# Loading q ahead of the raw token weights and rounding them between the first tiles' statistics, in an attention and MLP-mixer kernel

## The chip, the cores and the metric

The kernel runs on one core of one Trainium2 chip. The metric is the device time of one execution in microseconds (us). The core has a matrix engine (TensorE, PE in the profile), a vector engine (VectorE, DVE), an activation engine (ScalarE, ACT), GpSimd (POOL) and SyncE (SP), which here only issues transfers. "PEld" is the loading of weights into TensorE. Each engine runs its own instructions in order and waits on semaphores for the others. Transfers (DMA) are issued from a queue of SP, ScalarE or GpSimd and run on 16 DMA engines.

## The reference

```
kv  = einsum('bhsd,bhse->bhde', k, v)            # 8 batches, 8 heads, 576 rows, head size 64
o   = einsum('bhsd,bhde->bhse', q, kv)
o   = o / sqrt(mean(o*o, last axis) + 1e-6) * g_norm
x   = o, heads side by side                      # (8, 576, 512)
u   = x + (relu(x^T @ w_tok1) @ w_tok2)^T        # token mixing, 576 -> 256 -> 576
out = u + relu(u @ w_ch1) @ w_ch2                # channel mixing, 512 -> 1536 -> 512
```

The inputs q, k, v and g_norm are 32-bit floats; the four weights arrive as 64-bit floats and are rounded to 32 bits on the chip.

## The kernel before

The batches are worked on in four pairs. A pair has two sides, its two batches. A first stage (`start`) does the attention and part of the token mixing of pair 0. A second one (`middle`) finishes the token mixing of pair 0 beside the attention of pair 1. Two more (`steady`) and `last` follow in the same way, and after them comes the channel mixing, which takes most of the time. The change lies in the loads ahead of `start`, in `start` and in the first lines of `middle`.

The order of work is written out by hand. `start` and `middle` are lists of strings with short names of steps. `play` takes the names one by one and calls each step's function, and every instruction goes through `keep`, which holds it in that order on its engine. So on each engine the order of the strings is the order of execution. The names that matter here, with a tile c of two row blocks t (c = 0 and 1 are the two halves of side 0's 512 rows, 2 and 3 those of side 1, 4 the remainder, the last 64 rows of both sides):

- `kv{side}{half}`: k transposed times v for four of the eight heads, into PSUM (ps_kv, L133); `e{side}{half}` copies it to SBUF (kvp): on VectorE (L383) for side 0 of pair 0, otherwise on ScalarE (L130).
- `a{c}{t}`: q times kvp into a PSUM bank (ps_o, or ps_r for the remainder); there are two such banks in use.
- `g{c}{t}`: the bank times g_norm into x on VectorE (L444); `q{c}{t}`: its square on ScalarE (L448); `t{c}{t}`: the sum over a head on VectorE (L465); `m{c}`, `r{c}`, `i{c}`: mean (L470, VectorE), root (L475, ScalarE) and the inverse with one correction step (L479 to L484, four instructions on VectorE).
- `d{c}{t}` and `s{c}{t}`: x times that inverse, as one instruction on VectorE (L502) or as eight on ScalarE (L498).
- `h{side}{t}{j}`: one product of the first token weight, block t, with row block j of x, summed in a PSUM bank (ps_h); `h10` and `h11` are all four row blocks of side 1; `hr` is the part of the remainder, and the relu (L127) of all follows it.
- `w{n}{k}`: the rounding of weight block n. Blocks 0 and 1 are the two halves of w_tok1, 2 is its remainder, 3 and 4 are w_tok2. k = 0 loads the raw 64-bit words; 1 is two activations on ScalarE (L163 writes the scaled high word, L166 scales the low word in place); 2, 3 and 4 are a clamp (L169), a shift (L173) and an exact addition (L178) on VectorE.
- `j{n}`: n products of the identity with itself (ps_j) that nothing reads. They keep TensorE running.
- `l{side}{half}`, `lq`, `lr`: loads for the next pair, issued from SP.

A product of 32-bit floats is two passes in the profile. The loads of k, v, q and the raw weights are issued from SP in order (the first two of v from ScalarE). `load(n)` fetches k and v for half the heads of a batch, each as a transfer of 512 KB and one of 64 KB; `load_q(b)` fetches 1 MB of q; a raw block of w_tok1 is 512 KB. The transfers of the hardware queues use eight semaphores in turn, so one waits until that of eight places ahead has landed.

Of the kernel before, what the change touches and what calls it, by code (L numbers as in the profile page):

```python
# [20 lines left out]
def kernel(  # L21
# [90 lines left out]
    def do(f, *a, **kw):  # L112
        return lambda: f(*a, **kw)
# [6 lines left out]
    def dma(o, i, engine=nc.sync):  # L120
        keep(engine.dma_start(o, i))
# [16 lines left out]
    def load(n):  # L138

        if n >= 2 * B:  # L140
            return
        cols = [t[n // 2, :, ts(n % 2, DH)] for t in (k, v)]

        queues = (nc.sync, nc.scalar if n < 2 else nc.sync)
        for dst, c, e in zip((k_in[n % 4], v_in[n % 4]), cols, queues):
            dma(dst[:, :J], c[:LO].rearrange("(j p) e -> p j e", p=P), e)
            dma(dst[:HF, J], c[LO:], e)

    def load_q(b):
        if b < B:  # L150
            qT[b] = qtp.tile([P, HP, LO], F32, name="qT", tag="qT", bufs=2)
            dma(qT[b], q[b].rearrange("(c p) s -> p c s", p=P)[..., :LO])
# [69 lines left out]
    def get_ch2(f):  # L222

        a = 2 * (2 * f // NS)

        def loads(raw):
            t = raw.rearrange("p (h f n) w -> p f h n w", h=2, f=2)
            rows = words(moe_w_ch2)[ts(f, 2 * P)].rearrange("(f p) (h n) w -> f p h n w", f=2, h=2)
            return [(t[:, i], rows[i]) for i in range(2)]

        dst = w_ch2[:, a:a + 2, ds(2 * f % NS, 2)]
        return block(2 * DM, loads, dst.rearrange("p h f n -> p h (f n)"))
# [19 lines left out]
    def t_sums(b):  # L252

        def step(o, x, y):
            return lambda: tensor_add(b(o), b(x), b(y), ALU.subtract)

        return [step(5, 7, 1), step(6, 3, 5), step(7, 3, 7), step(4, 2, 6)]
# [934 lines left out]
    def play(lines, after={}, **stages):  # L1192

        for name in " ".join(lines).split():
            if name.isdigit():
                for _ in range(int(name)):
                    next(stages["rounding"], lambda: None)()
            elif name[0] == "-":  # L1200
                stages["before"][name[1:]]()
            else:
                next(stages[s][name] for s in ("attention", "mixing", "more")
                     if name in stages.get(s, ()))()
# [4 lines left out]
    channel = ([get_ch1(c, f) for f in range(2) for c in range(NC)]  # L1209
               + [get_ch2(f) for f in range(NF // 2)])  # L1210
    load(0)
    for block in tok1[:2]:
        block[0]()
    load(1)
    for t in [t for pair in zip(k_in, v_in) for t in pair]:
        keep(nc.gpsimd.memset(t[HF:, J], 0.0))
    zeroed = [ps["kv"].tile([P, 2, P], F32, name="ps_kv", tag="kv") for _ in range(2)]
    for t in zeroed:
# [5 lines left out]
    make_identity(nc, ident)  # L1224
    dma(g_sb, bass.AP(tensor=g_norm.tensor, offset=g_norm.offset,
                      ap=[[0, P], [0, 1], list(g_norm.ap[0])]), nc.scalar)
    load_q(0)
    for n in range(2, 4):
        load(n)
    load_q(1)  # L1230
# [2 lines left out]
    for block in tok1[2:] + tok2:  # L1233
# [5 lines left out]


    start = [
        "kv00 e00 l00 j14 w01 w11 w02 w03 w04 w12 w13 w14", "kv01 j10 e01 l01",
        "a00 g00 q00", "a01 g01 q01 t00 t01 m0", "a10 q10 r0 i0 d00 d01", "a11 q11 g10 g11 t10",
        "kv10 e10 t11 m1 r1", "h000 h010 h001", "kv11 e11 i1 d10 s11", "h011", "a20 q20",
        "a21 q21 g20 g21 t20 t21 m2", "h002 h012 r2 i2 d20", "a30 q30 g30", "a31 q31 s21 g31 t30", "h003 h013 t31 m3",
        "a40 q40 r3 i3 d30 s31 g40 t40 m4 r4 w21 i4 s40 lq0 l10 l11 lr0 lr1"]
    middle = [
        "kv00 e00 w31 w22 w23 w24", "h10 -lq1 w32 w33 w34", "kv01 e01 w41 w42",
        "h11 w43 w44", "hr l00", "a0 q00 g01 q01 g00 t00 t01", "u0 z2 f0", "u1 l01",
        "a1 q10 g11 q11 g10 t10 t11 m0 r0 lq0", "u2 i0", "kv10 e10 z4 d00", "u3 s01", "kv11 e11",  # L1250
        "u4 z6 f1", "a2 q20 g21 q21 g20 s10", "u5 t20 t21 f2", "a4 q40 g41 q41 g40 lr0 lr1 1", "u6 t40 t41 1 l10",
        "a3 q30 g31 q31 g30 lq1 d11", "u7 t30 t31 m2 r2 1 i2 p20 p21 s30", "u8 1 l11 d31"]
# [17 lines left out]
    more = {f"w{n}{k}": f for n, b in enumerate(tok1 + tok2) for k, f in enumerate(b)}  # L1270
# [6 lines left out]
    def keep_warm(n):  # L1277

        o = ps["h"].tile([P, DM], F32, name="ps_j", tag="h")
        for _ in range(n):  # L1280
            matmul(o[:, :P], lhsT=ident, rhs=ident, start=True, stop=True)

    more |= {f"j{n}": do(keep_warm, n) for n in (10, 14)}
    play(start, attention=attentions[0], mixing=mixings[0], more=more)
    play(middle, attention=attentions[1], mixing=mixings[0], before=attentions[0],
         more=more, rounding=rounding)
    for n in range(1, B // 2 - 1):
        play(steady[n - 1], attention=attentions[n + 1], mixing=mixings[n], before=attentions[n],
             more=more, rounding=rounding)
# [16 lines left out]
    more = {f"c{i}": f for i, f in enumerate(t_sums(lambda n: uT[0][:, SB[n]]))}  # L1306
# [97 lines left out]
```

## Time and profile before

| | |
|---|---|
| median of 3 runs | 788.1 us (786.69 to 788.41) |
| profiled execution, its own time | 787.48 us |
| its span | 785.7 us |
| TensorE busy | 773.3 us (98%) |
| VectorE busy | 614.8 us (78%) |
| ScalarE busy | 269.5 us (34%) |
| GpSimd busy | 71.3 us (9%) |
| granted TensorE clock | 1.0 |
| read from and written to HBM | 138.31 MB, 52.82 MB |

The span is the time from the first to the last instruction that the profile shows; the execution's own time is 1.8 us more. Busy shares are averages over the whole span. The first 60 us, with which the change has to do, look otherwise:

| stretch, us | PE busy | DVE busy | ACT busy | GB/s |
|---|---|---|---|---|
| 0 to 10 | 3.80 | 1.03 | 1.68 | 258 |
| 10 to 20 | 9.00 | 4.63 | 2.88 | 330 |
| 20 to 30 | 9.51 | 7.99 | 4.54 | 311 |
| 30 to 40 | 9.78 | 8.20 | 5.94 | 326 |
| 40 to 50 | 9.80 | 6.45 | 8.22 | 324 |
| 50 to 60 | 10.00 | 7.91 | 5.51 | 342 |

A row of the timeline gives start, duration, engine, line, operation, the tile written and the tiles read, shapes, how many instructions were merged, and in brackets how long the engine had been idle before and what ended the wait. The chain of waits is followed back from the last instruction: each piece is what the next one had to wait for.

### The profile page before, as it was taken

The numbers are of one execution on the slowest core, as the hardware profiler recorded it, in microseconds if no ns is written. First come the engines' busy times: TensorE is split into PE (matmuls) and PEld (weight loads), VectorE is DVE, ScalarE is ACT, GpSimd is POOL, SyncE is SP. The second block draws the span as 40 slices with busy tenths as digits, with TensorE's granted clock in tenths as the row PEclk, the third lists the DMA queues.
The fourth block names the chain that finished last, engine by engine and source line by source line (L and its number), as shares of the span: only waits on it lengthen the run. The fifth ranks groups of instructions, "written<-read, shape, count | busy, mean of one in ns | idle before, by whom it ended". The sixth has DMA issues, their size and how long they took to land.

```text
span 785.7 us, 14826 instructions
## 1 busy us (share of the span) xinstructions
PE 773.3 (98%) x5816; PEld 651.6 (83%) x5816; DVE 614.8 (78%) x909; ACT 269.5 (34%) x531; POOL 71.3 (9%) x84
## 2 busy tenths in 40 slices
PE   6999999999999999999999999999999999999998
PEld 6655545545888888999988899998889999889998
DVE  2877887795776868988778889776998885787977
ACT  2567463845110233521134242123352113325211
POOL 1001112123410000010100001010000101000111
PEclk9999999999999999999999999999999999999999
DMA  9999999787699795598897579889559989655864
GB/s 294 318 330 374 362 360 325 268 267 285 239 286 343 268 329 161 162 294 215 234 248 225 147 216 277 247 200 291 150 154 280 221 213 236 196 150 157 197 171 91
DMA packets 132613, 192.12 MB, mean 245 GB/s; under 512 B 13632, under 2 KB 92224, under 8 KB 132544
## 3 DMA queue, kind: packets, MB, share of 16 engines
q1 hardware_dynamic: 115984, 167.54, 67.8%
q0 software_dynamic: 14656, 22.02, 13.8%
q10 hardware_dynamic: 1904, 1.61, 0.7%
q8 instruction: 46, 0.75, 0.4%
q14 instruction: 23, 0.19, 0.1%
HBM read 138.31 MB, written 52.82 MB: 243 GB/s over the span
## 4 chain that ended last, share of the span: by engine, by line
PE 92%; ACT 3%; DVE 2%; DMA 2%; issue 0%; SPq 0%; ACTq 0%; DVEq 0%
PE ps_d L133 28%; PE ps_b L133 19%; PE ps_a L133 19%; PE ps_u L133 7%; PE ps_h L133 6%; PE ps_v L133 5%; PE ps_c L133 3%; PE ps_w L133 2%; PE ps_o L133 2%; PE ps_kv L133 2%; DMA raw<-in_moe_w_tok_dram 1%; ACT x L498 1%; DMA raw<-in_moe_w_ch_dram 1%; DVE ms L465 1%; DVE x L444 1%; ACT sq L448 1%
## 5 line engine op out<-in xcount | busy, mean ns | idle before, releaser
L133 PE MATMUL ps_d<-ui,w 128*128 128x256 f32 x504 | 118.7, 379 | 0.0
L130 ACT COPY ps_d<-ps_a 128x768 f32<-128x768 f32 (+1 forms) x56 | 32.0, 571 | 215.3 <-PE ps_a L133 215.3
L133 PEld LDWEIGHTS ps_d<-ui,w 128*128 128x128 f32 x504 | 95.1, 190 | 12.8 <-DVE v L124 0.2
L124 DVE TENSOR_TENSOR v<-v,v 128x1536 f32<-128x1536 f32 (+2 forms) x70 | 103.5, 1483 | 0.3
L133 PE MATMUL ps_b<-w,sv 128*128 128x128 f32 x672 | 84.6, 276 | 0.0
L133 PE MATMUL ps_a<-w,v 128*128 128x128 f32 x672 | 84.2, 275 | 0.0
L133 PEld LDWEIGHTS ps_a<-w,v 128*128 128x128 f32 x672 | 79.8, 192 | 0.2
L133 PEld LDWEIGHTS ps_b<-w,sv 128*128 128x128 f32 x672 | 79.5, 192 | 0.2
L133 PE MATMUL ps_u<-h,w_tok 128*128 128x512 f32 (+1 forms) x160 | 67.2, 606 | 0.8 <-ACT ps_u L130 0.7
L133 PE MATMUL ps_h<-x,w_tok 128*128 128x512 f32 (+1 forms) x160 | 65.6, 604 | 0.6 <-DVE x L502 0.4
L133 PE MATMUL ps_d<-w,v 128*128 128x128 f32 x528 | 66.2, 275 | 0.0
L133 PEld LDWEIGHTS ps_d<-w,v 128*128 128x128 f32 x528 | 62.7, 192 | 0.3
L127 ACT ACTIVATE v<-v 128x768 f32<-128x768 f32 (+1 forms) x54 | 42.6, 822 | 55.1 <-DVE v L124 55.1
L133 PE MATMUL ps_d<-w,sv 128*128 128x128 f32 x480 | 60.1, 275 | 0.0
L133 PEld LDWEIGHTS ps_d<-w,sv 128*128 128x128 f32 x480 | 57.1, 192 | 0.2
L133 PEld LDWEIGHTS ps_h<-x,w_tok 128*128 128x128 f32 (+1 forms) x160 | 26.0, 189 | 32.8 <-issue 27.6
L133 PEld LDWEIGHTS ps_u<-h,w_tok 128*128 128x128 f32 (+1 forms) x160 | 24.8, 179 | 31.5 <-issue 25.9
L1121 POOL DMA_DIRECT2D out_dram<-us x11 | 14.2, 1292 | 381.2 <-ACT us L130 268.9
L133 PE MATMUL ps_a<-uT,w 128*128 128x256 f32 x192 | 46.7, 379 | 0.0
L133 PE MATMUL ps_b<-ui,w 128*128 128x256 f32 x168 | 40.8, 379 | 0.0
L133 PEld LDWEIGHTS ps_a<-uT,w 128*128 128x128 f32 x192 | 36.3, 190 | 4.8
L444 DVE TENSOR_TENSOR x<-ps_o,g_sb 128x512 f32<-128x512 f32 x32 | 21.4, 687 | 23.7 <-PE ps_o L133 15.6
(145 smaller groups left out, 1213.0 us busy)
## 6 DMA issues: line engine op xcount, KB each, us to landing
w<-parts SPq DMA_DIRECT2D x168, 384.0 KB, 4.0
w<-parts SPq DMA_DIRECT2D x56, 192.0 KB, 3.0
uT<-blocks SPq DMA_DIRECT2D x36, 256.0 KB, 5.7
k_in<-in_k_dram SPq DMA_DIRECT2D x16, 512.0 KB, 9.0
qT<-in_q_dram SPq DMA_DIRECT2D x8, 1024.0 KB, 9.5
out_dram<-x POOLq DMA_DIRECT2D x16, 512.0 KB, 6.5
v_in<-in_v_dram SPq DMA_DIRECT2D x14, 512.0 KB, 9.1
raw<-in_moe_w_ch_dram SPq DMA_DIRECT2D x8, 768.0 KB, 10.5
```

Source lines behind the costliest of these rows:

```text
L124: keep(engine.tensor_tensor(out=o, in0=a, in1=b, op=op))
L127: keep(nc.scalar.activation(o, a, AF.Relu))
L130: keep(nc.scalar.copy(o, a))
L133: keep(nc.tensor.matmul(*a, **kw))
L444: keep(nc.vector.tensor_mul(x, bank[c, h], g_sb.to_broadcast([P, number(c), D])))
L448: keep(nc.scalar.activation(sq[c, h], bank[c, h], AF.Square))
L465: keep(nc.vector.tensor_reduce(stats_of(c)[0][:, h], sq[c, h], axis=AX.X, op=ALU.add))
L498: keep(nc.scalar.activation(x[:, k, h], x[:, k, h], AF.Copy, scale=inv[:, k, h]))
L1121: keep(nc.gpsimd.dma_start(to.rearrange("t p e -> p t e"), a, accum_op=ALU.add))
```

## The change

Ahead of `start`, the second k and v and the first q are loaded before the two raw blocks of w_tok1 in place of behind them.

In `start`, the rounding of the two halves of w_tok1 moves from the first line to between the statistics of tile 0 and tile 1. Row block 1 of tile 0 is scaled on ScalarE (`s01`) in place of VectorE (`d01`). The second group of identity products has 8 in place of 10, and a third group of 16 stands ahead of the first product with w_tok1. `kv10` moves behind that product.

In `middle`, `kv00` and `kv01` of pair 1 with their copies move from ahead of `h10` and `h11` to behind both, next to the remainder `hr`. The rounding steps beside them stay in order.

```diff
     load(0)
+    load(1)
+    load_q(0)
     for block in tok1[:2]:
         block[0]()
-    load(1)
...
-    load_q(0)
     for n in range(2, 4):
         load(n)
...
     start = [
-        "kv00 e00 l00 j14 w01 w11 w02 w03 w04 w12 w13 w14", "kv01 j10 e01 l01",
-        "a00 g00 q00", "a01 g01 q01 t00 t01 m0", "a10 q10 r0 i0 d00 d01", "a11 q11 g10 g11 t10",
-        "kv10 e10 t11 m1 r1", "h000 h010 h001", "kv11 e11 i1 d10 s11", "h011", "a20 q20",
-        "a21 q21 g20 g21 t20 t21 m2", "h002 h012 r2 i2 d20", "a30 q30 g30", "a31 q31 s21 g31 t30", "h003 h013 t31 m3",
+        "kv00 e00 l00 j14", "kv01 e01 l01 j8", "a00 g00 q00", "a01 g01 q01 t00 t01 m0 w01",
+        "a10 w02 w03 r0 q10 i0 d00 w04 w11", "a11 q11 s01 w12 w13 w14 j16", "h000", "kv10 e10 g10 g11 t10 t11 m1 r1",
+        "h010 h001 h011", "kv11 e11 i1 d10 s11", "a20 q20", "a21 q21 g20 g21 t20 t21 m2", "h002 h012 r2 i2 d20",
+        "a30 q30 g30", "a31 q31 s21 g31 t30", "h003 h013 t31 m3",
         "a40 q40 r3 i3 d30 s31 g40 t40 m4 r4 w21 i4 s40 lq0 l10 l11 lr0 lr1"]
     middle = [
-        "kv00 e00 w31 w22 w23 w24", "h10 -lq1 w32 w33 w34", "kv01 e01 w41 w42",
-        "h11 w43 w44", "hr l00", "a0 q00 g01 q01 g00 t00 t01", "u0 z2 f0", "u1 l01",
+        "h10 -lq1 w31 w22 w23 w24 w32", "h11 w33 w34 w41 w42", "kv00 kv01 e00 e01 w43 w44", "hr l00", "a0 q00 g01 q01 g00 t00 t01", "u0 z2 f0", "u1 l01",
...
-    more |= {f"j{n}": do(keep_warm, n) for n in (10, 14)}
+    more |= {f"j{n}": do(keep_warm, n) for n in (8, 14, 16)}
```

## The prediction

> **What bounds the kernel now.** First the page, for who is busy and what the last chain consists of:
>
> ```profile
> span 785.7 us, 14826 instructions
> PE   6999999999999999999999999999999999999998
> PE 92%; ACT 3%; DVE 2%; DMA 2%; issue 0%; SPq 0%; ACTq 0%; DVEq 0%
> ```
>
> TensorE is full in every slice but the first. Between 42 us and the end its single passes leave only three gaps over 0.1 us: 0.24 at 69.3, 0.12 at 105.9 and 0.66 at 148.7. So a delay before 42 us should reach the end nearly whole, and all edits of work lie there. Second, the chain of waits of the first 60 us (start, us, what):
>
> ```profile
> 2.49 9.63 DMA raw<-in_moe_w_tok_dram
> 12.14 0.68 ACT w_tok L163
> 12.84 0.71 DVE w_tok L178
> ...
> 13.95 1.39 PE ps_kv L133 x40
> 15.33 2.43 PE ps_j L133 x20
> ...
> 23.11 0.70 DVE x L502
> ...
> 23.86 2.84 PE ps_h L133 x6
> 26.70 1.32 PE ps_kv L133 x40
> ...
> 39.51 2.03 ACT x L498 x8
> ...
> 41.58 1.12 PE ps_h L133 x2
> ```
>
> It begins with the raw token weights and ends with the last scaling, s31 (39.51), for which `h10`'s fourth tile waits. Between 30.95 and 41.5 only VectorE and ScalarE carry it. The 13.95 is laid to L178; the k of `kv01` was issued at 6.12 and took 7.7 us, so it landed at 13.86 and held `kv01`. Third, the timeline of the two places that decide; TensorE beside the remainder and ScalarE ahead of the second pair of tiles:
>
> ```profile
> 36.29 1.09 PE L133 MATMUL ps_r<-kvp,qR 128*64 128x128 f32 x16 [0.22 <-DVE x L444]
> 37.22 1.35 PE L133 MATMUL ps_kv<-v_in,k_in 128*64 128x64 f32 x40
> 38.50 2.88 PE L133 MATMUL ps_h<-x,w_tok 128*128 128x512 f32 x6
> 41.58 1.12 PE L133 MATMUL ps_h<-x,w_tok 128*128 128x512 f32 x2 [0.20 <-ACT x L498]
> 42.63 1.39 PE L133 MATMUL ps_kv<-v_in,k_in 128*64 128x64 f32 x40
> ```
>
> ```profile
> 28.06 0.37 ACT L130 COPY kvp<-ps_kv 128x256 f32<-128x256 f32 x1 [0.81 <-PE ps_kv L133]
> 28.33 2.02 ACT L498 ACTIVATE x<-x,inv 128x64 f32<-128x64 f32 x8
> 30.25 1.30 ACT L448 ACTIVATE sq<-ps_o 128x512 f32<-128x512 f32 x2
> ```
>
> Pair 1's `kv00` (37.22) fills time in which `h10` would wait anyway: only 0.20 us is idle at 41.58. ScalarE does e11, s11, q20 in a row, and e11 starts when `kv11` ends.
>
> [...]`ps_j` passes start 0.213 us apart until 11.5 us, 0.112 after.[...] From 3 to 6 us the two queues had 50.0% and 57.7% of the engines[...].
>
> **The change, step by step.** *q in front.* SP's queue is now k0, k1, q0, raw0, raw1. `kv00` (6.20) and the 14 `ps_j` matmuls to 13.40 stand as before: k0 and v0 are first in both queues. v1 is untouched on ScalarE's queue and landed by 2.76+8.4 = 11.2. k1 takes raw0's place, which landed at 1.87+7.9 = 9.8. Both are before 13.40, so `kv01` starts there: -0.55. The 8 `ps_j` that follow instead of 10 save 2x0.223 = 0.45. So `a00` starts at 16.60 in place of 17.59: -0.99. q landed at 16.7 with 1 MB of raw ahead; at the 329 GB/s of this stretch that is 3.2 us, so now about 13.5. Were it as late as 16.7, a00 would lose 0.1; were k1 as late as 13.9, 0.5. raw0 and raw1, 1 MB behind q, land by about 16.7, before their use at 19.8. The loads k2 to q1 each wait for the landing of the DMA eight places ahead (eight semaphores are used in turn) and come at the same times within a us; their users start 5 us later. I take 0 for that.
>
> *Rounding between statistics.* It was seven VectorE instructions at 10.51 to 15.27, free under the warming matmuls; now it has to come before `h000`. Up to m0 all moves by -0.99: g00 17.70, q01 19.32, m0's end 20.84, a11's end on TensorE 21.06. VectorE: w02 and w03 (0.43 each) to 21.76, the four steps of i0 (22.12 to 23.08 before) from 21.79, d00 at 22.78, w04 (0.70) from 23.39 to 24.09. ScalarE: w01 19.83 to 21.06, r0 and q10 to 21.70; then w11. In the built program its L163 waits for w04's L178 (both write `w_tok1`), so it runs 24.12 to 25.36, and behind it stand q11 (to 25.86), s01 (8 activations, 2.02, to 27.79), e10, r1, e11, s11. s01 replaces d01, 0.6 us of VectorE. VectorE then does w12 to w14 until 26.52, g10, g11, t10, t11 (2.5 us) and i1, until d10's end at 31.09.
> TensorE: 16 `ps_j`, 32 passes of 0.112 and 0.1 to begin, fill 21.06 to 24.73, 0.64 beyond w04. Without them h000 could start at 24.13; the wait for w04 would stand there in their place. h000 0.96, `kv10` 1.31 (it filled the wait for d00 before), h010, h001, h011 2.77 (as 23.86 to 26.63), `kv11` from 29.77: its end is 31.2 where it was 28.06. h010's wait (w14) and h001's (s01, 27.79 against 27.96) are just covered; if s01 is 1 us later, 0.8 is lost there.
> e11 31.21, s11 31.48 to 33.50, q20 33.40, g20 34.01 against 30.86: +3.15. q21 no longer trails a21: -0.1. From there to s31 instructions and order are the same, so `h10`'s fourth tile starts at 41.58+3.05 = 44.63.
>
> *kv00 and kv01 of the second pair.* Both now come behind `h11`. Their time is the same, but kv00's 1.32 us leaves the wait for s31 and comes after it. The remainder starts at 39.3 (g30), `h10` waits about 1.2 us for d30 and 0.4 for s31; nothing is left to put there. +1.32. Were TensorE the late one there, it would be 0. e00 and e01 go behind w31, w41 on ScalarE, with `hr` (2.07 us) between them and `a0`: 0. The later k_in reload waits for kv00 (about 50 in place of 38.5), but SP comes to it at 48.7 only, so 1 to 2 us on a load used near 100: 0. One raw block of the channel weights goes behind a uT load near 164 on SP, for a rounding with slack: 0 to 0.3.
>
> Sum: 3.05+1.32 = +4.37. Less what the gap of 0.66 at 148.7 takes up, which follows a load on saturated DMA: 0 to 0.66, I take 0.3. +4.1 us on the profiled execution's 787.48 us (span 785.7 and 1.8 around it): 791.6. The median of the three runs is 788.1, so 792.2.
>
> **The rivals.** A, the sum: 792.2 (791.6 to 792.7), 0.66. B, the stage is TensorE's and not VectorE's: the kv move is free, +2.7 to 3.1: 791.0. For it: only 0.20 us idle at 41.58. Against it: 10 us of the chain without TensorE. 0.14. C, the clock: in 38.0 to 44.6 TensorE would be idle some 3 of 6.7 us in pieces of at most 1.4[...]: 793.9 to 795.6.[...] 0.10. D, the other side: the 0.99 us at a00 carries through and the rounding stays hidden: 788.1-1.0 = 787.1. It needs e11 over by 28.43-0.99 = 27.4; w11 behind w04 would have to cost nothing, and TensorE would have to take h000 by 21.6 (23.86-0.99, less kv10's 1.31 that now follows). The 16 `ps_j` alone end at 24.7. A part of it, the range of +-1.6 us, is as likely. 0.05 each. That q does not come earlier (the change not doing what it says) costs 0.1 as above and is inside A.
>
> **How the numbers follow.** Likeliest A: 792.2. What a measurement can tell from no change is about 0.2%, 1.6 us. 8 in 10: from B's low side, 790.3, to C's middle, 794.5; outside are D and C's upper half. Faster 0.05, same 0.05, slower 0.90.
>
> **What would show it.** a00 near 16.6 and kv01 near 13.4 (q in front right). On ScalarE, L163 idle for about 2.4 us on w04's L178, and L498 of c0 before the first kvp copy. h000 after 24 us, the second kvp1 copy near 31.2, g20 near 34. ps_h idle on L498 by 1 us or more after ps_r, and kv twice in a row behind it. A from 50 us on parallel course, 4.4 us later. The prediction is wrong if e11 is before 30, if `h10` does not wait for s31, if ps_h passes near 45 us come at half rate, or if later gaps take up over 0.7 us.

## The result and the profile after

The changed kernel took 791.1 us (median of 5, 790.86 to 791.87) where the kernel before took 787.02 in the same comparison (5 runs, 786.52 to 788.41). The ratio is 1.0049 with a 95% interval of 1.0036 to 1.0063: the change costs about 4 us (2.8 to 5.0). The profiled execution took 790.89 us, its span is 789.1.

The page of the changed kernel, span, slices of TensorE and the engines' shares of the last chain:

```profile
span 789.1 us, 14890 instructions
PE   6999999999999999999999999999999999999998
PE 96%; ACT 1%; DVE 1%; DMA 1%; issue 0%; ACTq 0%
```

TensorE has risen from 92% to 96% of the chain. About 7 us of that rise lie in the first 62 us, where the chain now runs over all three groups of `ps_j` and no longer over the raw weights and their rounding. Most of it, about 23 us, lies later: from 127.8 to 153.9 us the chain of before ran over VectorE, ScalarE and a load of channel weights, and there TensorE had the gap of 0.66 us at 148.7; in the changed kernel only 3.1 us of the chain around that place (149.7 to 152.8) are not TensorE's. The slices look the same; 3.4 us in 789 can't be seen in them.

The chain of waits of the changed kernel (start, us, what):

```profile
0.75 5.31 DMA v_in<-in_v_dram
...
8.55 5.11 PE ps_j L133 x28
13.66 1.32 PE ps_kv L133 x40
14.97 1.98 PE ps_j L133 x16
...
19.26 2.05 PE ps_o L133 x16
21.31 3.57 PE ps_j L133 x32
24.88 0.86 PE ps_h L133 x2
...
29.83 1.34 PE ps_kv L133 x40
...
42.51 2.03 ACT x L498 x8
...
44.58 4.56 PE ps_h L133 x10
49.14 2.48 PE ps_kv L133 x80
```

The raw weights and their rounding (2.49 to 13.55 in the chain before) are gone from it. `kv01` follows `j14` without a gap. But 3.57 us of identity products now lead up to `h000`, and the chain still ends in the stage with s31 (42.51, before 39.51), 3.00 us later.

The timeline of the two places shown before; TensorE beside the remainder, and ScalarE ahead of the second pair of tiles:

```profile
39.30 1.09 PE L133 MATMUL ps_r<-kvp,qR 128*64 128x128 f32 x16 [0.79 <-DVE x L444]
40.32 1.98 PE L133 MATMUL ps_h<-x,w_tok 128*128 128x512 f32 x4
43.25 1.12 PE L133 MATMUL ps_h<-x,w_tok 128*128 128x512 f32 x2 [0.95 <-DVE x L502]
44.58 4.56 PE L133 MATMUL ps_h<-x,w_tok 128*128 128x512 f32 x10 [0.20 <-ACT x L498]
49.07 2.55 PE L133 MATMUL ps_kv<-v_in,k_in 128*64 128x64 f32 x80
```

```profile
24.05 0.67 ACT L163 ACTIVATE w_tok<-raw 128x512 f32<-128x512 f32 x1 [2.23 <-DVE w_tok L178]
...
25.66 2.01 ACT L498 ACTIVATE x<-x,inv 128x64 f32<-128x64 f32 x8
...
31.19 0.37 ACT L130 COPY kvp<-ps_kv 128x256 f32<-128x256 f32 x1 [1.90 <-PE ps_kv L133]
31.46 2.02 ACT L498 ACTIVATE x<-x,inv 128x64 f32<-128x64 f32 x8
33.38 1.05 ACT L448 ACTIVATE sq<-ps_o 128x512 f32<-128x512 f32 x2
```

The 1.35 us of `kv00` that stood between the remainder and `h10` is missing there, and 0.95 of idling at 43.25 has come in its place; both kv groups follow at 49.07. ScalarE stands idle for 2.23 us ahead of w11's L163, and e11, s11, q20 come 3.13 us after their times before (28.06, 28.33, 30.25).

Last, three rows of VectorE's timeline in the changed kernel show where the rounding now is: w04's addition behind d00, w12 after a wait for w11, and only then tile 1's first product with g_norm:

```profile
23.33 0.69 DVE L178 CUSTOM_DVE_ANT_1 w_tok<-w_tok,raw 128x1024 uint16<-128x1024 uint16 x1
24.75 0.43 DVE L169 TENSOR_SCALAR w_tok<-w_tok 128x512 f32<-128x512 f32 x1 [0.74 <-ACT w_tok L163]
...
26.36 1.28 DVE L444 TENSOR_TENSOR x<-ps_o,g_sb 128x512 f32<-128x512 f32 x2
```

The balance, by the trace: +3.00 us at h10's fourth tile (44.58 against 41.58), +3.97 at `a0` (53.47 against 49.50), then the gap of 0.66 at 148.7 has shrunk to 0.12, and TensorE's last product ends at 785.86 against 782.45: +3.41.

### The profile page after: what moved, and what is told of

Its sections match the earlier page's. It is cut to its first block, busy times and chain, and to the rows that moved or that the text cites. A ratio compares the mean times of both kernels' runs of the same rounds, so it can differ in the third digit from the quotient of the medians.

```text
span 789.1 us, 14890 instructions
## 1 busy us (share of the span) xinstructions
PE 776.8 (98%) x5844; PEld 654.8 (83%) x5844; DVE 613.7 (78%) x908; ACT 271.3 (34%) x539; POOL 71.3 (9%) x84
## 3 DMA queue, kind: packets, MB, share of 16 engines
q0 software_dynamic: 14656, 22.02, 13.5%
## 4 chain that ended last, share of the span: by engine, by line
PE 96%; ACT 1%; DVE 1%; DMA 1%; issue 0%; ACTq 0%
PE ps_d L133 28%; PE ps_b L133 19%; PE ps_a L133 19%; PE ps_u L133 8%; PE ps_h L133 7%; PE ps_v L133 5%; PE ps_kv L133 3%; PE ps_c L133 3%; PE ps_w L133 2%; PE ps_o L133 2%; PE ps_j L133 1%; ACT x L498 1%; DMA v_in<-in_v_dram 1%; DVE ms L465 0%; DVE x L444 0%
```

## The experiments

One thing has to be taken out before traces are compared. TensorE began at half rate (`ps_j` passes start 0.213 us apart, later 0.112), and the moment at which it went to full rate differed from execution to execution: `j14`, the same 14 products in the same place, ended at 13.40 in the profiled execution before, at 13.66 after, and between 12.34 and 13.61 in the ten below. Where TensorE or the statistics set the pace, all that follows moves along with it. So the table counts h10's fourth tile from j14's end; `a0` is counted from the fourth tile. Where a load sets the pace, this count misleads, since the load did not move with j14: with the loads in the order of before (before, kv move alone, loads in the old order) the k of `kv01` landed at 13.65 to 14.05 where j14 ended at 12.84 to 13.60, and `kv01` waited for it. Each row's last two columns come from one profiled execution.

| kernel | median us | ratio to before, 95% | fourth tile after j14 | a0 behind it |
|---|---|---|---|---|
| before | 787.0 to 787.8 | | 28.18 | 7.92 |
| after | 791.1 | 1.0049 (1.0036 to 1.0063) | 30.92 | 8.89 |
| kv move alone | 788.61 | 1.0008 (0.9998 to 1.0019) | 28.78 | 8.89 |
| first stage alone | 789.92 | 1.0025 (1.0016 to 1.0034) | 30.93 | 7.92 |
| w11 ahead of w04 | 791.46 | 1.0043 (1.0027 to 1.0060) | 30.93 | 8.89 |
| kv10 back | 790.95 | 1.0041 (1.0027 to 1.0055) | 30.80 | 8.89 |
| both | 790.1 | 1.0030 (1.0020 to 1.0041) | 29.74 | 8.89 |
| no third identity group | 791.29 | 1.0042 (1.0027 to 1.0057) | 31.92 | 8.89 |
| 8 in it instead of 16 | 790.62 | 1.0049 (1.0029 to 1.0068) | 30.81 | 8.89 |
| loads in the old order | 792.23 | 1.0055 (1.0041 to 1.0069) | 31.90 | 8.89 |
| rounding early | 788.21 | 1.0005 (0.9997 to 1.0014) | 28.96 | 7.81 |
| rounding early, square first | 788.1 | 1.0010 (1.0002 to 1.0017) | 29.54 | 7.90 |

An interval reaches 0.6 to 1.5 us to either side, so a step of a few tenths is read from the traces and not from the medians.

### The two halves of the change

The kernel before, with only the kv groups of `middle` moved:

```diff
-        "kv00 e00 w31 w22 w23 w24", "h10 -lq1 w32 w33 w34", "kv01 e01 w41 w42",
-        "h11 w43 w44", "hr l00",
+        "h10 -lq1 w31 w22 w23 w24 w32", "h11 w33 w34 w41 w42", "kv00 kv01 e00 e01 w43 w44", "hr l00",
```

> The kernel before with only the second pair's kv00 and kv01 moved behind h11. Theory A (the chain through VectorE and ScalarE up to s31 sets when h10's fourth tile can start; kv00's 1.32 us only filled a wait): h10's fourth tile still starts at 41.6 us, TensorE is idle some 1.5 us between the remainder and it (0.2 before), a0 of pair 1 starts at 50.8 in place of 49.5, and the end is 0.7 to 1.3 us later (ratio to before 1.0009 to 1.0017). Theory B (TensorE sets this stage, the move is free): no idle time beyond 0.3 us there, a0 at 49.5, ratio 1.000.

TensorE's timeline of that kernel:

```profile
41.05 1.12 PE L133 MATMUL ps_h<-x,w_tok 128*128 128x512 f32 x2 [0.95 <-DVE x L502]
42.38 4.56 PE L133 MATMUL ps_h<-x,w_tok 128*128 128x512 f32 x10 [0.20 <-ACT x L498]
46.87 2.55 PE L133 MATMUL ps_kv<-v_in,k_in 128*64 128x64 f32 x80
```

The wait for d30 (0.95) appears where `kv00` was taken away, in a first stage that is otherwise the old one. `a0` comes 8.89 us after the fourth tile where it was 7.92: the move costs 0.97. (I had expected 1.5 us of idling and a cost of 1.3; the waits are 0.95 and 0.20.) All eight traces with the moved groups show 8.89, the other four 7.81 to 7.92. TensorE's last product ends at 783.68, 1.23 us after that of before; the rest of it is the fourth tile, which came at 42.38 and not 41.58, mostly since j14 ended 0.20 later and `a20` waited 0.37 for q's second load; 0.54 is taken back at the later gap. The median is 0.9 us above before in an interval that just includes no difference, so it is the trace that settles this one.

The other half, the changed kernel with the old `middle`:

```diff
-        "h10 -lq1 w31 w22 w23 w24 w32", "h11 w33 w34 w41 w42", "kv00 kv01 e00 e01 w43 w44", "hr l00",
+        "kv00 e00 w31 w22 w23 w24", "h10 -lq1 w32 w33 w34", "kv01 e01 w41 w42",
+        "h11 w43 w44", "hr l00",
```

> The changed kernel with the second pair's kv00 and kv01 back where they were. Theory A: h10's fourth tile starts at 44.6 us as in the changed kernel, the idle time ahead of it falls from 1.15 us to about 0.2, a0 of pair 1 starts at 52.2 (53.5 in the changed kernel, 49.5 before), and the end is 2.1 to 2.7 us later than before (ratio 1.0027 to 1.0035). Theory B: the first stage is the whole cost, a0 at 53.5, ratio 1.0045 to 1.005.

Its fourth tile comes 30.93 us after j14's end, as in the changed kernel, and `a0` 7.92 behind it, as in the kernel before. So the halves add in the traces: the first stage costs 2.75 us and the kv move 0.97. The medians (0.9 and 2.2 us above before, each in its own comparison) fit that once the 0.54 of the later gap is taken off, within their intervals.

### What holds the first stage: w11, kv10, or both

The changed kernel with w11 ahead of w04:

```diff
-        "a10 w02 w03 r0 q10 i0 d00 w04 w11", "a11 q11 s01 w12 w13 w14 j16", "h000", "kv10 e10 g10 g11 t10 t11 m1 r1",
+        "a10 w02 w03 r0 q10 i0 d00 w11 w04", "a11 q11 s01 w12 w13 w14 j16", "h000", "kv10 e10 g10 g11 t10 t11 m1 r1",
```

> The changed kernel with w11 ahead of w04 in the list, so that ScalarE's second L163 need not wait for L178. Theory A (TensorE's order, 16 identity products and kv10 behind h000, makes kv11 late): L163 starts near 21.8 in place of 24.05, q11 and s01 are over some 2 us earlier, w14 0.8 us earlier, but h000 stays at 24.7, kv11 ends at 31.15 and g20 starts at 34.0 as in the changed kernel; time unchanged (ratio to before 1.0043 to 1.005). Theory W (the wait of w11, with q11, s01, e10 and e11 queued behind it, is what makes the second pair of tiles late): e11 and g20 come 0.8 to 2 us earlier and the time falls by that, ratio 1.0025 to 1.004.

L163 now follows q10 at once (20.63, where 22.98 would answer to the changed kernel's 24.05, as this execution runs 1.07 ahead), s01 is over at 24.24 and w14 at 24.67. The fourth tile is where it was, to 0.01 us. The 2.23 us for which ScalarE waits are real, and alone they set nothing. (The profiled execution of this kernel shows 1.75 us of idle TensorE in `a0` at 53.2, ended by nothing that the profile shows. The next kernel but one has 0.72 at the same place, the others none. I have no cause for it.)

Then `kv10` back in front of `h000`, w11 left where the change put it (this was run after the kernel with both edits, which follows below; the expectation refers to it):

```diff
-        "a10 w02 w03 r0 q10 i0 d00 w04 w11", "a11 q11 s01 w12 w13 w14 j16", "h000", "kv10 e10 g10 g11 t10 t11 m1 r1",
+        "a10 w02 w03 r0 q10 i0 d00 w04 w11", "a11 q11 s01 w12 w13 w14 j6 kv10 j4", "h000", "e10 g10 g11 t10 t11 m1 r1",
```

> The changed kernel with kv10 back ahead of h000 (6 identity products, kv10, 4 more, then h000), w11 left behind w04. With w11 moved as well the fourth tile came 1.2 us sooner. A: here w11's wait keeps w14 to 26.4 and s01 to 27.7, so h010 waits at about 25.7 and h001 to 27.7, kv11 starts at about 29.5, and 0.3 us at most is won: h10's fourth tile 30.6 to 30.9 us after j14's end, 790.8 to 791.1. Rival, w11's place never matters: 1.2 us is won as with both, 29.7 after j14's end, 789.9.

TensorE's timeline of it:

```profile
21.92 1.39 PE L133 MATMUL ps_kv<-v_in,k_in 128*64 128x64 f32 x40
23.24 1.16 PE L133 MATMUL ps_j<-ident 128*128 128x128 f32 x8
24.23 1.02 PE L133 MATMUL ps_h<-x,w_tok 128*128 128x512 f32 x2
25.74 3.19 PE L133 MATMUL ps_h<-x,w_tok 128*128 128x512 f32 x6 [0.48 <-DVE w_tok L178]
```

Only 0.12 us is won: `h010` now waits for w14 (the 0.48), and a second pause follows for s01. Both edits together:

```diff
-        "a10 w02 w03 r0 q10 i0 d00 w04 w11", "a11 q11 s01 w12 w13 w14 j16", "h000", "kv10 e10 g10 g11 t10 t11 m1 r1",
+        "a10 w02 w03 r0 q10 i0 d00 w11 w04", "a11 q11 s01 w12 w13 w14 j6 kv10 j4", "h000", "e10 g10 g11 t10 t11 m1 r1",
```

> The changed kernel with w11 ahead of w04, and kv10 ahead of h000 again: 6 identity products, kv10, 4 identity products fill the time that 16 took. Theory A: h000 at 24.8, kv11 ends at 29.9 (31.15 in the changed kernel), g20 starts at 32.75, h10's fourth tile at 43.3; 1.2 to 1.3 us faster than the changed kernel, ratio to before 1.0027 to 1.0036. Theory W alone (kv10's place does not matter): the same as the run with w11 ahead of w04 alone. If kv11's place is not what sets g20, the time stays at the changed kernel's.

Its TensorE from the same place on:

```profile
22.04 1.39 PE L133 MATMUL ps_kv<-v_in,k_in 128*64 128x64 f32 x40
23.36 1.16 PE L133 MATMUL ps_j<-ident 128*128 128x128 f32 x8
24.35 3.68 PE L133 MATMUL ps_h<-x,w_tok 128*128 128x512 f32 x8
27.96 1.39 PE L133 MATMUL ps_kv<-v_in,k_in 128*64 128x64 f32 x40
```

The four products run through, and 1.18 us is won. 0.00 and 0.12 alone, 1.18 together: in the changed kernel `kv11` has two causes that end about 0.1 us apart, TensorE's own row of work (`kv10` behind `h000`) and w14 with s01 behind the wait on ScalarE. It takes both away to gain.

### The third group of identity products

```diff
-        "a10 w02 w03 r0 q10 i0 d00 w04 w11", "a11 q11 s01 w12 w13 w14 j16", "h000", "kv10 e10 g10 g11 t10 t11 m1 r1",
+        "a10 w02 w03 r0 q10 i0 d00 w04 w11", "a11 q11 s01 w12 w13 w14", "h000", "kv10 e10 g10 g11 t10 t11 m1 r1",
```

> The changed kernel without its third group of 16 identity products. Up to a11's end (about 21.1 us) nothing changes. A (the sum): the 3.7 us of ps_j only cover the wait for w04, so h000 starts when w04's L178 ends, 24.0 instead of 24.7; h010 then waits for w14 (26.4) and h001 for s01 (27.7), so kv11 starts at about 29.5 and h10's fourth tile comes at most 0.3 us earlier than in the changed kernel (44.58 there, 30.92 after j14's end): 790.8 to 791.1. C (the clock): an idle TensorE of 2.7 us ahead of h000 and more behind lets the clock fall, the ps_h passes of h000 to h011 start over 0.4 us apart instead of 0.24, and kv11 and all behind it come 1 to 3 us later: 792 to 794.

TensorE's timeline of it:

```profile
23.24 1.72 PE L133 MATMUL ps_h<-x,w_tok 128*128 128x512 f32 x2 [2.75 <-DVE w_tok L178]
24.89 2.35 PE L133 MATMUL ps_kv<-v_in,k_in 128*64 128x64 f32 x40
27.17 2.84 PE L133 MATMUL ps_h<-x,w_tok 128*128 128x512 f32 x6
```

My expectation A was wrong here, and C right in its mechanism, at the low end of its size. `h000` and `kv10` take 1.65 and 2.28 us from start to start, where they took 0.96 and 1.31; the pairs of passes of `kv10` start 0.107 us apart instead of 0.058. The passes of `h010` behind it are back at full rate. The granted clock says the same: over stretches of one us it reads 0.50 from 24 to 27 us, and the trace's record of its changes has the half rate from 23.63 to 27.04. So after 2.75 us without a product TensorE ran at half rate for 3.41 us, and the fourth tile came 1.00 us later than with the group.

The medians don't show the 1.00 us: this kernel's ratio is 1.0042, that of the changed kernel 1.0049. Nor does the fall seem to come every time. The mean granted clock of its four runs is 0.998, 1.000, 0.997 and 0.997, where the five of the changed kernel have 1.000, and the run at 1.000 (791.27 us) lies among the other three (790.92 to 791.56). So the 1.00 us is what the fall cost in one execution.

How much idling is too much was asked with 8 products in place of 16:

```diff
-        "a10 w02 w03 r0 q10 i0 d00 w04 w11", "a11 q11 s01 w12 w13 w14 j16", "h000", "kv10 e10 g10 g11 t10 t11 m1 r1",
+        "a10 w02 w03 r0 q10 i0 d00 w04 w11", "a11 q11 s01 w12 w13 w14 j8", "h000", "kv10 e10 g10 g11 t10 t11 m1 r1",
```

> The changed kernel with 8 identity products in its third group instead of 16. With none TensorE was idle for 2.75 us ahead of h000, then h000 and kv10 took 1.72 and 2.35 us in place of 1.1 and 1.39, and the fourth tile came 31.9 us after j14's end instead of 30.9. Here it is idle for about 1 us. If only a long idle piece slows it: h000 at the end of w04 (24.0 on the changed kernel's time), passes at full speed, h010 then waits for w14 and h001 for s01, and h10's fourth tile comes 30.7 to 30.9 us after j14's end: 790.8 to 791.1. If 1 us is enough: passes of h000 at half speed and 31.4 or more, 791.5 and over.

Its TensorE:

```profile
24.03 1.13 PE L133 MATMUL ps_h<-x,w_tok 128*128 128x512 f32 x2 [0.97 <-DVE w_tok L178]
25.09 1.39 PE L133 MATMUL ps_kv<-v_in,k_in 128*64 128x64 f32 x40
```

After 0.97 us the rate holds, and `h000` comes at w04's end (24.03). Of the 0.6 us that it gains only 0.11 is left at the fourth tile, as the first of the two expectations had it: w14 and s01 are next. So 8 of the 16 products were enough to keep the rate here; fewer than 8, but some, was not tried.

### What the order of the loads is worth

The changed kernel with the loads in the order of before:

```diff
     load(0)
-    load(1)
-    load_q(0)
     for block in tok1[:2]:
         block[0]()
+    load(1)
...
+    load_q(0)
     for n in range(2, 4):
         load(n)
```

> The changed kernel with the loads in the order of before (raw token weights first, then the second k and v, q last); start and middle as changed. A: q lands at 16.7 instead of 13.8, k1 at about 13.9, so a00 starts at about 17.6 instead of 16.8 and all that hangs on tile 0's statistics comes 0.5 to 0.9 us later, h10's fourth tile 31.4 to 31.8 us after j14's end: 791.6 to 792.0. So q in front is worth 0.5 to 0.9 us by itself, and the place of the rounding costs 3.5. Rival, the early q gains nothing since the raw weights come later for it: same as the changed kernel, 791.1, or sooner, down to 790, w01 being held by nothing.

TensorE's timeline of it:

```profile
13.74 1.39 PE L133 MATMUL ps_kv<-v_in,k_in 128*64 128x64 f32 x40 [0.90 <-issue]
```

`kv01` waits 0.90 us behind `j14`, until its k has landed (13.65), and the fourth tile comes 0.98 later after j14's end than in the changed kernel (31.90 against 30.92). So the order of the loads does what it was reckoned to do, but its worth is no single number: the k lands when it lands, wherever j14 ends. With j14 over at 12.84, as here, the old order costs 0.98 us; in the kernel before, with j14 over at 13.40, `kv01` waited 0.55; with 13.66, the profiled execution of the changed kernel, 0.1 to 0.4 would be left, as the k lands at 13.65 or 13.86. In us from the start the fourth tile comes at 44.74 here and at 44.58 there. And what was won here is the earlier k: q landed at 16.62, before `a00` could use it (16.95). What q's own place adds is not shown by any run.

Counted from `kv01`, which leaves the loads out, the fourth tile comes 31.00 us later here, 30.99 in the changed kernel and 27.63 in the kernel before. So the new order of `start` by itself costs about 3.4 us, and between the profiled executions of before and after the loads gave back 0.62 of it.

Would such a start be a gain over the kernel before, if the rounding were kept out of the way? The raw weights now land at 15.3 and 16.8, while VectorE and ScalarE wait for `a00`. This kernel rounds the first half right then, puts `kv10` and `kv11` back in their old places with 4 identity products instead of 16, and keeps the old `middle`:

```diff
-        "kv00 e00 l00 j14", "kv01 e01 l01 j8", "a00 g00 q00", "a01 g01 q01 t00 t01 m0 w01",
-        "a10 w02 w03 r0 q10 i0 d00 w04 w11", "a11 q11 s01 w12 w13 w14 j16", "h000", "kv10 e10 g10 g11 t10 t11 m1 r1",
-        "h010 h001 h011", "kv11 e11 i1 d10 s11", "a20 q20", "a21 q21 g20 g21 t20 t21 m2", "h002 h012 r2 i2 d20",
+        "kv00 e00 l00 j14", "kv01 e01 l01 j8 w01 w02 w03 w11 w04",
+        "a00 g00 q00", "a01 g01 q01 t00 t01 m0", "a10 w12 r0 q10 i0 d00 w13 w14", "a11 q11 s01 g10 g11 t10 j4",
+        "kv10 e10 t11 m1 r1", "h000 h010 h001", "kv11 e11 i1 d10 s11", "h011",
+        "a20 q20", "a21 q21 g20 g21 t20 t21 m2", "h002 h012 r2 i2 d20",
```

> q in front as in the change, but the first half's rounding (w01, w02, w03, w11, w04) ahead of tile 0's statistics, in the time when VectorE and ScalarE are free, the second half's w12 beside r0 and w13, w14 behind d00; 4 identity products in place of 16, kv10 ahead of h000 and kv11 ahead of h011 as before; s01 on ScalarE; middle as before. Theory 1, the first stage is then bound by q's second load, which landed at 28.0 to 29.6 in all kernels so far: a20 waits for it and starts at 28.9 to 29.7, h10's fourth tile at 41.6 to 42.3, no gain over the kernel before: 787.0 to 788.4. Theory 2, the 0.8 us gained at a00 goes through to the end once the rounding is out of the way: a20 at 28.1, 786.2.

Nearly all of the loss is gone (788.21 us), and nothing is won. How much each of the edits gives back can't be told from this kernel. `a20` starts at 28.93, as in the kernel before (28.91). It waited for q there, if only for about 0.2 us: it comes 1.19 us behind `h011`'s start, where the kernel before has 0.96, and 0.14 behind the landing of q's second load (28.79). But q00 (18.81), late behind g00, which stood behind w04 and so behind w11, had kept TensorE idle for 1.17 us ahead of `a10` (0.52 in the kernel before), so there was little left for that load to hold. The next kernel takes that wait away by putting w04 behind g00:

```diff
-        "kv00 e00 l00 j14", "kv01 e01 l01 j8 w01 w02 w03 w11 w04",
-        "a00 g00 q00", "a01 g01 q01 t00 t01 m0", "a10 w12 r0 q10 i0 d00 w13 w14", "a11 q11 s01 g10 g11 t10 j4",
+        "kv00 e00 l00 j14", "kv01 e01 l01 j8 w01 w02 w03 w11",
+        "a00 g00 w04 q00", "a01 g01 q01 t00 t01 m0", "a10 w12 r0 q10 i0 d00 w13 w14", "a11 q11 s01 g10 g11 t10 j4",
```

> The kernel with the early rounding, with one step put back: w04 behind g00 instead of ahead of it, so that g00 and q00 do not wait for w11 and w04 (there q00 came at 18.8 and a10 waited 1.2 us for it). a10 then starts at about 18.7, all up to h011 some 0.7 us sooner. Theory 1, a transfer bounds the stage's end: a20 waits for q's second load (28.8 there) and kv00 of pair 1 for its v (38.2 there), and nothing is won: 787.4 to 788.4, h10's fourth tile 42.0 to 42.3. Theory 2, VectorE and ScalarE bound it: a20 at 28.2, the fourth tile at 41.5, 787.0 to 787.5.

TensorE's timeline of it:

```profile
27.37 1.12 PE L133 MATMUL ps_h<-x,w_tok 128*128 128x512 f32 x2
29.11 2.02 PE L133 MATMUL ps_o<-kvp,qT 128*128 128x128 f32 x16 [0.61 <-DMA qT<-in_q_dram]
...
37.88 1.39 PE L133 MATMUL ps_kv<-v_in,k_in 128*64 128x64 f32 x40 [0.22 <-DMA v_in<-in_v_dram]
```

`h011` is done 0.37 us earlier than in the kernel above, and `a20` starts later, at 29.11: it waits 0.61 us for q's second load, and `kv00` of pair 1 waits for its v. (I had expected the wait of `a10` to go. It was 1.65 us, because w11 itself waited for its raw block and ran to 18.55, ahead of q00. That j14 ended at 12.34, earliest of all, gave the head start, and not the edit.) Theory 1 holds at this point: what was gained in front was lost at `a20`. In four kernels (kv move alone, both, and the two with early rounding) `a20` came 0.13 to 0.14 us behind the landing of q's second load, at 28.9 to 29.6; in the twelve traces that load landed at 27.8 to 29.9. Neither of these kernels beats the one before, whose `a20` at 28.91 was already within 0.9 us of q's landing (28.04). In the kv move alone, which has the first stage of before, `a20` waited for that load (0.37 us): in some executions the old first stage already stands at this bound.

## Why the prediction was right

The likeliest case, A, was right in its mechanism, its places and nearly in its size: 791.1 us measured, 792.2 predicted, slower and inside the range of 790.3 to 794.5, though below A's own 791.6 to 792.7. The change itself was put at 4.1 us. By the medians it is 4.1 (791.1 less 787.02), by the two profiled executions 3.4, and 3.3 to 3.6 against the medians of the kernel before in the later comparisons (787.5 to 787.8). So that the 4.1 was hit exactly is in part luck. Two ends of the range don't follow from the sums beside them: B's low side is 788.1 and 2.7, 790.8 and not 790.3, and the middle of C is 794.75. The measured time lies inside either way.

**q in front.** k1 and v1 had landed by 10.7, q at 13.8 (13.5 in the prediction), the raw blocks at 15.3 and 16.8. `kv01` had no gap: that 0.55 came from k1, and the q at 13.8 lay three us ahead of its use, as the prediction's own 0.1 for a late q implied. `a00` started at 16.79, not 16.60; from j14's end it is 3.13 us, predicted 3.20. The loads behind it did not come at quite the same times: q's second load landed at 29.14 instead of 28.04, 1.1 us later, where the prediction took nothing. It had cover in the changed kernel, whose `a20` came at 31.08, so nothing was lost; in the kernels with early rounding it bounds.

**Rounding between statistics.** w04 ended at 24.01 (24.09 predicted), L163 waited 2.23 us for it (2.4), `h000` came at 24.72 (24.73), `kv11` at 29.76 (29.77), e11 at 31.19 (31.21), g20 at 33.99 (34.01), the fourth tile at 44.58 (44.63). That these agree to 0.1 us flatters the prediction: j14 ended 0.26 later than assumed, and counted from there three steps up to `h000` were about 0.1 shorter each (30.92 to the fourth tile where the sum gives 31.23). The statement that w14 and s01 were "just covered" is what the experiments with w11 and `kv10` showed as two causes of nearly one length.

**kv00 and kv01.** The wait came where it was said, for d30 and for s31, but at 0.95 and 0.20 us and not 1.2 and 0.4, with 0.79 at the remainder. The term was mis-sized: 0.97 us and not 1.32. The sum moved `kv00` at the price of a group between products with 512 columns. Behind one another the two groups take 2.48 us from start to start, 1.16 more than the one group in that place before, and the remaining products lose a change of shape (6.41 us in place of 6.60; the pass before such a change takes 0.52 us and the one behind it 0.53, the others 0.43): 1.16 less 0.19 is 0.97.

**The gap at 148.7** took up 0.54, inside the 0 to 0.66 given, where 0.3 was taken. The load ahead of it took from 130.93 to 136.65 in the kernel before, and from 127.8 to 144 the 16 DMA engines were busy for 0.96 of the time. The two terms make the difference: 4.37 less 3.97 and 0.54 less 0.3 are together 0.64 of the 0.7 us between 791.6 and the profiled 790.89.

**The rivals.** B gave 791.0, which is where the median is, but by the wrong way: it has the kv move free, and the trace of that move alone shows the wait and the 0.97 us. C did not happen: `ps_h` passes at 43.25 and 44.58 go at full rate, and TensorE was idle for 1.94 us in three pieces there rather than some 3. What idling would cost by way of the rate was an estimate of the author's, which no trace had shown by then. The danger was real at another place, ahead of `h000`: with the 16 identity products, or with 8 of them, the passes there go at full rate, and the prediction counted them as a filler that only stands in place of a wait. Their removal cost 1.00 us in the profiled execution. D fell at the point it named: `h000` at 24.7 instead of 21.6, e11 at 31.2 instead of 27.4.

Why the change costs time at all: the rounding ran on VectorE from 10.5 to 15.3 (six instructions, not the seven I had counted), when VectorE had nothing else to do, and now stands between the statistics of tile 0 and `h000`, which waits for w04. `kv10`, which had filled a wait, follows behind `h000` instead. Taking back the kv move is worth 0.97 us, and the edits of w11 and `kv10` together 1.18; what is left of the loss went when the first half's rounding was moved early, but no run moved the rounding alone, so its own share is not shown. What the loads bring is real (0.62 us between the two profiled executions), and smaller than the 3.4 that the new order of `start` costs.

## What to carry to other kernels

A load brought forward pushed others back here (the raw blocks landed at 15.3 and 16.8 us instead of 9.8 and 12.1), and the work behind such a one moves with it: look up whether its engine had free time at the old place and has any at the new one. Where one start has two causes of nearly one length, taking either away shows nothing; take both before you say that neither matters. Before you count a step from a mark, ask whether what sets the pace moves with that mark: the k of `kv01` (13.65 to 14.05 in the old order) did not move with the moment at which TensorE went to full rate. Before you give an early start a value, look for the next transfer on its way: here the stage could not gain more than the 0.9 us between q's second landing and its use.

## What the runs showed of the hardware

- The moment at which TensorE went to full rate was not fixed. The record of the granted clock has it between 9.49 and 12.26 us in twelve profiled executions (in the kernel before `ps_j` passes start 0.213 us apart up to 11.7 us and 0.112 from there, in the changed kernel up to 12.3), and the same products ended between 12.34 and 13.66, a spread of 1.3 us at the head of the chain, about a third of the change's whole effect.
- An idle piece of 2.75 us (no third identity group) was followed by half rate; pieces of 0.97 (8 in it), of 1.65 (ahead of `a10` in the last kernel), of 1.75 (in `a0`, w11 ahead of w04), and of 0.79, 0.95 and 0.20 within 6.1 us (the changed kernel), were not. The granted clock of the whole execution moved only to 0.998, since 3.41 us at half rate take 0.2% off the mean of 790; over stretches of one us it reads 0.50. Why one of the four runs without the third group shows no fall (1.000) was not shown: no trace of that run was kept.
- The last of the 16 completions of q's second load came 1.0 to 1.8 us behind the others: 15 lay between 26.29 and 27.08 us in the kernel before and the last at 28.04; between 26.32 and 27.36 and at 29.14 in the changed kernel; between 26.6 and 27.4 and at 28.8 with early rounding, where `a20` started 0.14 us behind the last.
